# Pooled attention of a fused attention and MoE kernel: 112 + 32 keys per head on array tiles in place of block-diagonal weights

## The chip, the cores and the metric

One NeuronCore of a Trainium2 chip. The time of a kernel is the device time of one execution in microseconds (us), as the median of the runs of one session. The engines are named as in the profile: PE (TensorE matmul), PEld (its weight load), DVE (VectorE), ACT (ScalarE), POOL (GpSimd), SP (SyncE, which here only issues DMAs).

## The reference

The kernel computes an attention layer for 8 batches of 8 heads (576 positions, 64 per head) and, on its output, a gated feed-forward layer of 4608 tokens, 512 wide inside and out, 1536 in the middle. Attention is the sum of two: a pooled one over groups of four positions, and a local one within a distance of 3.

```python
def _attn_ref(q, k, v):
    B, H, S, D = q.shape                       # 8, 8, 576, 64
    factor, scale = 4, 1.0 / np.sqrt(D)
    Sd = S // factor                           # 144 pooled positions
    ...                                        # sm_attn: softmax(scale * q k^T) v
    q_d = q.reshape(B, H, Sd, factor, D).mean(axis=3)   # k_d, v_d alike
    out_up = np.repeat(sm_attn(q_d, k_d, v_d), factor, axis=2)
    mask = np.abs(pos[:, None] - pos[None, :]) < factor
    ...                                        # masked softmax of q k^T, times v
    return out_up + out_local

def _moe_ref(x, w_gate, w_val, w_out):
    gate = np.maximum(x @ w_gate, 0.0)
    return gate * (x @ w_val) @ w_out
```

## The kernel before

**Order.** Nothing is scheduled by the compiler: every engine runs its instructions in the order in which they are emitted, and that order is one long list of tokens, `SEQ` (2338 of them). A token such as `scores/a/0@2` names a step, a pair of heads and a chunk of tokens, and calls one function. The 64 heads are worked on as 32 pairs (two heads side by side: head 0 on partitions 0 to 63, head 1 on 64 to 127); the feed-forward layer works on nine chunks of 512 tokens, and its matmuls (L951, L1295, L1199, L1036) are interleaved token by token with the attention of pairs further on. Four pairs are worked on for each chunk.

**Pairs before the twelfth** use an older form. Their local scores and pooled scores are matmuls over 64 rows, one per head (L621 for the pooled ones with 72 keys, L632 for the local ones, each head in a PSUM bank of its own). Pairs 0 to 3 form their output on other lines (L669, L681); pairs 4 to 7 have denominators and numerators for two heads on 64 columns each (L722, L731, L743, L752). Q and K of the first pairs are turned by matmuls with 64 output columns (L549).

**Pairs from the twelfth on** (`NEW = 12`, twenty pairs) treat both heads in one matmul over all 128 rows, with block-diagonal weights: a weight tile that holds head 0 in its upper left and head 1 in its lower right quarter, zeros elsewhere.

- Loads: Q and K by GpSimd's DMA queue, turned by a DMA transpose on SP's queue (`emit_qkT`, L529). V comes twice: for the local part in fp16 (`emit_load_vb`), and for the pooled part in fp32 (`emit_load_v4`, L520), on SP's queue. Rows 0 to 47 of that tile hold head 0, rows 64 to 111 head 1, each row 12 consecutive positions, so three pooled keys (w = 0, 1, 2).
- Pooling: Q and K by a reduction on VectorE (`emit_pool`, L536) into `qkd`, [128, 2, 144]; V by two additions on GpSimd (`emit_v2`, L573, then `emit_v1`, L581, two instructions of 48 partitions) into `vp`, three block-diagonal weight tiles. K is copied by ScalarE (`emit_kd`, L806, one copy per head) into `kd`, again three block-diagonal tiles of 2 x 48 keys.
- Scores (`emit_scores`): four matmuls for the pooled part (L836: 144 columns for w = 0 and w = 1, 72 for each half of w = 2), then ten for the local part (L840). `flat` is all of PSUM as one row of 8 banks of 512; the pooled results lie at 0 to 215 and 798 to 1013 from the start of bank 4, the local ones between.
- Exponentials on ScalarE (`emit_exp_st`, `emit_exp_pool`), a mask on VectorE (`emit_mask_st`).
- Output (`emit_out_st`): step 0 is `emit_pooled` twice, first for the denominator (weights `four_st`, a block of fours that is loaded from a constant), then for the numerator (weights `vp`), three matmuls of 144 columns each (L867). Step 1 is the local denominator (L882), steps 2 and 3 the local numerator (L887). Then logarithm, inverse and product (`emit_ln_st`, L899; `emit_inv`, L920; `emit_xn_st`, L902) and the sum of the two attentions (`emit_xsum_st`).

Zeros that the block-diagonal tiles need are written once by `emit_zero` (kinds `d` and `v` on VectorE, L813), and tokens `const/2`, `zero/d/*`, `zero/v/*` and `kd/*` in `SEQ` place these steps.

```python
        for w, o, a, n in ((0, 0, 0, SD), (2, SD, 0, 72), (1, 798, 0, SD), (2, 798 + SD, 72, 72)):
            nc.tensor.matmul(
                out=flat[:, lo + o : lo + o + n], lhsT=kd[r2][:, w, :], rhs=qd[:, a : a + n], start=True, stop=True
            )
```

Of the kernel before, what the change touches and what calls it, by code (L numbers as in the profile page):

```python
# [43 lines left out]
next/0/1@0 vd/7/4 qk/b0/1@0 qk/a1/1@0 hg/11/*/7 relu/11/7 next/1/1@0 flip/9 hv/11/*/0 p/1/0@1 gate/11/0 sumhi/0/0@1
v/a/1@0 vc/7/4 num/7/1/7 tr/8/0/1 keep/1/0@1 zero/b/6 ev/8/01A/1 wt/1 v/b/0@0 num/7/0/6 tr/8/1/0 wt/2 den/7/0/4
den/7/1/5 ln/4 sumhi/1/0@1 p/2/0@1 c11//0@1 zs/1.1/0@1 qk/b2/0@1 qk/b2/1@0 p/6/0@1 vd/8/5 ev/8/00A/1 inv xn/6
p/5/0@1 next/0/0@1 keep/2/0@1 vc/8/5 ev/8/10A/0 p/7/0@1 ev/8/11A/0 scores/a/0@1 exp/a1/0@1 xsum/7 keep/3/0@1
hg/0/0@1 qk/b3/1@0 hv/0/0@1 wt/3 relu/0/0@1 qk/a0/0@1 flip/10 qk/a2/0@1 mask/a1/0@1 hg/2/0@1 next/2/0@1 sum/3/0@1
ed/a/0@1 o/a11/0@1 c22//0@1 exp/a0/0@1 mask/a0/0@1 next/1/0@1 p/4/0@1 o/a01/0@1 qk/a3/0@1 zs/1.0/0@1 tn/1/0@1
gate/0/0@1 c21//0@1 o/a10/0@1 ln/a1/0@1 p/3/0@1 flip/11 next/3/0@1 qk/b3/0@1 c12//0@1 relu/2/0@1 qk/b1/0@1 o/a00/0@1  # L50
ln/a0/0@1 inv/a/0@1 pool/b/0@1 xn/a1/0@1 hg/1/0@1 relu/1/0@1 zero/b/1 v2/a/1@1 hg/4/0@1 zero/b/5 hv/1/0@1 gate/1/0@1
hv/2/0@1 xn/a0/0@1 qk/b0/0@1 vd/9/7 vc/9/7 hg/3/0@1 relu/3/0@1 flip/12 gate/2/0@1 xsum/a/0@1 zs/2.0/0@1 scores/b/0@1
exp/b0/0@1 mask/b0/0@1 exp/b1/0@1 mask/b1/0@1 qk/a3/1@1 hv/3/0@1 gate/3/0@1 vd/10/2 ed/b/0@1 zs/3.0/0@1 vc/10/2
# [10 lines left out]
qk/b2/1@1 hg/4/1@1 hg/5/1@1 qk/b1/0@2 xsum/a/1@1 inv/b/1@1 xn/b1/1@1 v/b/0@1 xn/b0/1@1 kd/a1/1@1 v2/b/1@1 v4/b/1@1
qk/b0/0@2 hv/4/1@1 kd/a0/1@1 relu/5/1@1 relu/4/1@1 gate/4/1@1 hv/5/1@1 gate/5/1@1 zero/b/4 v/b/1@1 zero/k/1
qk/b3/0@2 qk/b2/0@2 xsum/b/1@1 up/2.1/0@2 xq/0/0@2 xq/1/0@2 kk/b0/0@2 sq/4.0.0.1/0@2 xq/2/0@2 scores/a/0@2
vh/10.6/0@2 uk/2.1/0@2 sk/4.0.0.1/0@2 sq/4.0.0.2/0@2 sq/4.0.0.5/0@2 sq/4.0.0.6/0@2 sumhi/0/0@2 kk/b1/0@2 vh/4.7/0@2
sf/4.0.0.11/0@2 xq/3/0@2 sk/4.0.0.2/0@2 v2/a/0@2 sq/4.0.0.3/0@2 next/0/1@1 sk/4.0.0.5/0@2 sq/4.0.0.7/0@2 up/2.5/0@2
sumhi/1/0@2 exp/a0/0@2 ed/a/0@2 next/1/1@1 kk/a1/0@2 sf/4.0.0.22/0@2 sq/4.0.0.4/0@2 sf/4.0.0.21/0@2 mask/a0/0@2
sf/4.0.0.12/0@2 gt/4.7.0/0@2 up/2.6/0@2 uk/2.2/0@2 uk/2.5/0@2 sq/0.0.2.1/0@2 sq/0.0.2.5/0@2 sk/0.0.2.5/0@2 sum/2/0@2  # L70
sum/3/0@2 gt/10.6.1/0@2 o/a00/0@2 o/a01/0@2 up/2.7/0@2 sk/0.0.2.1/0@2 uf/2.22/0@2 sq/0.0.2.6/0@2 sk/0.0.2.2/0@2
ln/a0/0@2 inv/a/0@2 pool/b/0@2 next/0/0@2 up/2.2/0@2 o/a10/0@2 sq/0.0.2.3/0@2 sq/0.0.2.2/0@2 sf/0.0.2.11/0@2
sq/0.0.2.7/0@2 v1/a/0@2 after/3/0@2 sf/0.0.2.22/0@2 sf/0.0.2.12/0@2 kd/b0/0@2 o/a11/0@2 xn/a0/0@2 up/2.4/0@2
# [1550 lines left out]
```

## Time and profile before

| | |
|---|---|
| median of 3 runs | 343.01 us (342.77 to 344.65) |
| span of the profiled execution, first to last instruction | 341.8 us |
| the profiled execution's own time | not listed apart from its span; the median of the runs is 1.2 us above it |
| busy in the span | PE 331.0 (97%), DVE 292.9 (86%), ACT 272.1 (80%), POOL 188.6 (55%) |
| instructions | 9062, of them 3410 matmuls |
| granted TensorE clock | 1.00 |
| DMA | 43.91 MB in 162176 packets; HBM read 46.59 MB, written 9.44 MB |

A row of a group reads: line, engine, operation, output and inputs by name, rows*columns of the weight tile, shape, type, count, then busy time of the group, mean ns of one, and idle time of the engine before them with what ended it. A row of the timeline reads: start, length, engine, line, operation, names, shape, count; neighbours of one form are merged. The duration of a matmul goes from its start to the modelled end of its results, and the next one may start well before that. The rows themselves stand in the prediction.

### The profile page before, as it was taken

The page shows a single profiled execution, that of the slowest core. Times are in us where ns is not written, and L with a number is a line of the kernel's source. Part 1 is how long each engine was busy: PE and PEld are TensorE (multiplying, and loading weights), DVE is VectorE, ACT ScalarE, POOL GpSimd, SP SyncE. Part 2 cuts the span into 40 slices and gives each one's busy share as a digit, 9 for nine tenths or more (in the row PEclk, how much of TensorE's full clock was granted, in tenths as well). Part 3 has the DMA queues.
Part 4 walks back from the last instruction along what each step waited for, and adds up shares of the span by engine and source line. Part 5 has one row for each costly group of instructions (what it writes and reads, how often), then busy time and mean ns, then how long its engine had stood idle before and what let it go on. Part 6 is the DMA issues. An engine that isn't in the chain of part 4 may idle for free.

```text
span 341.8 us, 9062 instructions
## 1 busy us (share of the span) xinstructions
PE 331.0 (97%) x3410; PEld 243.5 (71%) x3410; DVE 292.9 (86%) x578; ACT 272.1 (80%) x653; POOL 188.6 (55%) x268
## 2 busy tenths in 40 slices
PE   7899999999999999999999999999999999999995
PEld 3765556657457786878677868787778768888874
DVE  6694689999999898989899989998998898897692
ACT  3878787799997998889889888988898647896842
POOL 8993655929998669849985698675510000000000
PEclk9999999999999999999999999999999999999999
DMA  9999999999999999999999999999300102003013
GB/s 135 165 170 208 185 194 167 150 186 148 168 187 133 192 88 218 128 185 105 220 118 194 92 191 151 189 122 190 51 33 1 63 2 93 3 15 109 3 56 130
DMA packets 162176, 43.91 MB, mean 128 GB/s; under 512 B 147500, under 2 KB 156820, under 8 KB 162132
## 3 DMA queue, kind: packets, MB, share of 16 engines
q0 software_dynamic: 123136, 19.51, 79.5%
q1 hardware_dynamic: 38884, 23.80, 32.3%
q8 instruction: 26, 0.43, 0.5%
q14 instruction: 18, 0.15, 0.1%
q10 hardware_dynamic: 112, 0.02, 0.0%
HBM read 46.59 MB, written 9.44 MB: 164 GB/s over the span
## 4 chain that ended last, share of the span: by engine, by line
PE 79%; DMA 6%; DVE 5%; POOL 4%; ACT 3%; issue 2%; DVEq 0%; ACTq 0%; POOLq 0%
PE ps L1295 24%; PE ps L951 24%; PE ps L1199 17%; DMA qk<-in_k_dram 3%; PE ps L1036 3%; DMA wv_sb<-in_moe_w_val_dram 3%; PE ps L867 2%; POOL qk L463 2%; PE ps L840 2%; PE ps L887 1%; PE ps L882 1%; POOL vw L513 1%; PE ps L836 1%; DVE xo L1030 1%; DVE xT L1175 1%
## 5 line engine op out<-in xcount | busy, mean ns | idle before, releaser
L951 PE MATMUL ps<-xT,wv_sb 128*128 128x512 f16 x352 | 89.4, 379 | 0.0
L951 PEld LDWEIGHTS <-wv_sb 128*128 128x128 f16 x352 | 32.5, 97 | 27.5
L468 POOL DMA_DIRECT2D qk<-in_k_dram x46 | 33.6, 732 | 19.3 <-DMA qkT<-qk 16.3
L1390 DVE SCALAR_TENSOR_TENSOR gT<-r,ps 128x512 f16<-128x512 f16 x55 | 37.5, 682 | 6.1 <-PE ps L951 5.1
L1295 PE MATMUL ps<-xT,qk 128*128 128x256 f16 x240 | 40.9, 272 | 0.0
L468 POOL DMA_DIRECT2D qk<-in_q_dram x46 | 34.0, 740 | 12.1 <-DMA qkT<-qk 7.1
L1306 ACT COPY ps<-ps 128x256 f32<-128x256 f32 x80 | 29.0, 366 | 8.1 <-PE ps L1295 7.4
L1295 PE MATMUL ps<-xT,wg_sb 128*128 128x256 f16 x180 | 33.9, 272 | 1.1 <-DVE xT L1313 0.6
L536 DVE TENSOR_REDUCE qkd<-qkT 128x288 f16<-128x1152 f16 x23 | 30.8, 1338 | 0.0
L486 POOL DMA_DIRECT2D vw<-in_v_dram x40 | 28.9, 732 | 2.3 <-DMA qk<-in_q_dram 1.7
L1311 ACT CAST r<-ps 128x256 f16<-128x256 f32 x55 | 20.2, 367 | 11.0 <-DVE r L1313 6.3
L581 POOL TENSOR_TENSOR vd<-v 48x192 f16<-48x192 f32 x40 | 26.0, 650 | 1.7
L1210 ACT COPY ps<-ps 128x256 f32<-128x256 f32 x54 | 19.4, 366 | 9.1 <-PE ps L1199 7.3
L951 PE MATMUL ps<-xT,wg_sb 128*128 128x512 f16 x104 | 26.1, 380 | 0.5 <-ACT r L960 0.5
L1295 PEld LDWEIGHTS <-qk 128*128 128x128 f16 x240 | 22.2, 97 | 4.8
L573 POOL TENSOR_TENSOR v<-v 112x384 f32<-112x384 f32 (+1 forms) x21 | 22.6, 1074 | 4.0 <-DMA v<-in_v_dram 3.6
L1295 PEld LDWEIGHTS <-xo 128*128 128x128 f16 x240 | 22.5, 97 | 2.9 <-DVE xo L1030 0.2
L1295 PEld LDWEIGHTS <-wg_sb 128*128 128x128 f16 x180 | 17.0, 97 | 10.7 <-issue 3.1
L1295 PE MATMUL ps<-wt,xo 128*128 128x256 f16 x180 | 24.5, 272 | 0.0
L920 ACT ACTIVATE rden<-rden 128x720 f32<-128x720 f32 x28 | 22.5, 803 | 0.8
L1313 DVE TENSOR_TENSOR r<-ps,xT 128x256 f16<-128x256 f32 x44 | 18.1, 418 | 4.4 <-PE ps L1295 3.1
L963 DVE TENSOR_TENSOR gT<-r,ps 128x512 f16<-128x512 f16 x24 | 16.1, 679 | 6.0 <-PE ps L951 3.2
(181 smaller groups left out, 883.8 us busy)
## 6 DMA issues: line engine op xcount, KB each, us to landing
out_dram<-y_sb SPq DMA_DIRECT2D x24, 256.0 KB, 3.8
v<-in_v_dram SPq DMA_DIRECT2D x20, 192.0 KB, 5.1
qk<-in_k_dram POOLq DMA_DIRECT2D x46, 72.0 KB, 5.6
qk<-in_q_dram POOLq DMA_DIRECT2D x46, 72.0 KB, 5.2
vw<-in_v_dram POOLq DMA_DIRECT2D x38, 80.0 KB, 4.5
v<-in_v_dram SPq DMA_DIRECT2D x20, 144.0 KB, 5.2
out_dram<-y_sb SPq DMA_DIRECT2D x22, 128.0 KB, 1.8
vw<-in_v_dram POOLq DMA_DIRECT2D x12, 168.0 KB, 6.2
```

Of the source, the lines that this page charges most:

```text
L468: nc.gpsimd.dma_start(dst.rearrange("p (j h d) -> p j h d", h=2, d=64)[:, :, hh, :], _dap(src, off + hh * S * D, [[D, 96], [NQ * D, NB], [ ...
L486: nc.gpsimd.dma_start(t[lo : lo + 64, j0:j1, lo : lo + 64], _dap(v, base + j0 * QB * D, [[D, 64], [QB * D, j1 - j0], [1, D]]),)
L536: nc.vector.tensor_reduce(out=qkd[hp % 2].rearrange("p i t -> p (i t)"), in_=qkT[hp % 4][:, 0 : 2 * S].rearrange("p (t f) -> p t f", f=4), ...
L573: nc.gpsimd.tensor_tensor(out=m, in0=t[:, :, 0:128], in1=t[:, :, 128:256], op=ALU.add)
L581: nc.gpsimd.tensor_tensor(out=vp[hp % 3][lo : lo + 48, :, lo : lo + 64], in0=m[:, :, 0:64], in1=m[:, :, 64:128], op=ALU.add)
L920: nc.scalar.activation(out=rden, in_=rden, func=AF.Exp, scale=-1.0)
L951: nc.tensor.matmul(out=out, lhsT=w[:, kk, bass.ts(jj, 128)], rhs=xT[:, kk, c * TCH : (c + 1) * TCH], start=(kk == 0), stop=(kk == 3),)
L1199: nc.tensor.matmul(out=out, lhsT=self.left[i][t], rhs=self.right[i][t], start=(i == 1 and t == 0), stop=(t == n - 1), skip_group_check=True,)
L1295: nc.tensor.matmul(out=out, lhsT=self.left[i - 1][k], rhs=self.right[i - 1][k], start=(i == 1 and k == 0), stop=(k == n - 1), skip_group_c ...
L1306: nc.scalar.copy(out=o, in_=x)
L1311: nc.scalar.copy(out=o, in_=self.d if i == 11 else self.a)
L1390: lambda c, jj, b, t: nc.vector.scalar_tensor_tensor(out=gT[c % 2][:, jj, :], in0=tg[t], scalar=0.0, in1=ps[:, b, :], op0=ALU.max, op1=ALU ...
```

## The change

For the twenty pairs from the twelfth on, the pooled part no longer uses block-diagonal tiles. Each head's 144 pooled keys are split into 112 and 32.

- Scores: one matmul per head over its own 64 rows for 112 keys (144 columns), and for the last 32 keys two per head (72 columns, one for each half of the queries), head 0 to partitions 0 to 31, head 1 to 32 to 63. Six matmuls in place of four, with weights straight from `qkd`; `emit_kd`, `kd` and its zeros go.
- Output: denominator and numerator have one matmul per head over 112 keys, to 64 columns each, and one per head over 32 keys on 32 rows. Eight matmuls in place of six. Weights of the denominator are a part of `ones_sb` that is there already (`four_st` and its load go).
- V for the pooled part: 112 partitions with both heads side by side, and 32 partitions per head for the rest: three loads in place of two, rows of 1 KB in place of 3 KB. `emit_v1` is one instruction of 112 partitions in place of two of 48.
- The exponential of the pooled scores covers 112 partitions, and two memsets at the start clear what no load fills. Of the 14 first warming matmuls, one each goes to banks 4 and 5. 48 tokens leave `SEQ`; the order of the others is unchanged.

```diff
+    MK = 112
+    RK = SD - MK
...
-    vp = [t.rearrange("p (w k) -> p w k", k=128) for t in vdfull]
+    vp = [t[:, 0:192].rearrange("p (w d) -> p w d", d=64) for t in vdfull]
...
+        for t in v4n:
+            nc.vector.memset(t[64:MK, 512:768], 0.0)
...
         if hp >= NEW:
+            t = v4n[hp % 2]
+            nc.sync.dma_start(
+                t[0:MK, 0:512].rearrange("p (h x) -> p h x", h=2),
+                _dap(v, off, [[4 * D, MK], [S * D, 2], [1, 4 * D]]),
+            )
             for hh in range(2):
-                lo, n = 64 * hh, 64 - 16 * hh
                 nc.sync.dma_start(
-                    v4n[hp % 2][lo : lo + n], _dap(v, off + hh * S * D, [[12 * D, n], [1, 12 * D]])
+                    t[RK * hh : RK * hh + RK, 512:768],
+                    _dap(v, off + hh * S * D + 4 * MK * D, [[4 * D, RK], [1, 4 * D]]),
                 )
...
         if hp >= NEW:
-            for lo in (0, 64):
-                m = v2full[hp % 2][lo : lo + 48, 0:3]
-                nc.gpsimd.tensor_tensor(
-                    out=vp[hp % 3][lo : lo + 48, :, lo : lo + 64], in0=m[:, :, 0:64], in1=m[:, :, 64:128], op=ALU.add
-                )
+            m = v2full[hp % 2][0:MK, 0:3]
+            nc.gpsimd.tensor_tensor(out=vp[hp % 3][0:MK], in0=m[:, :, 0:64], in1=m[:, :, 64:128], op=ALU.add)
...
-    def emit_kd(hp, hh):
-        lo = 64 * hh
-        nc.scalar.copy(
-            out=kd[hp % 2][lo : lo + 64, :, lo : lo + 48],
-            in_=qkd[hp % 2][lo : lo + 64, 1, :].rearrange("p (k w) -> p w k", w=3),
-        )
...
-        qd = qkd[r2][:, 0, :]
-        for w, o, a, n in ((0, 0, 0, SD), (2, SD, 0, 72), (1, 798, 0, SD), (2, 798 + SD, 72, 72)):
+        heads = [qkd[r2][64 * hh : 64 * hh + 64] for hh in range(2)]
+        for hh, d in enumerate(heads):
             nc.tensor.matmul(
-                out=flat[:, lo + o : lo + o + n], lhsT=kd[r2][:, w, :], rhs=qd[:, a : a + n], start=True, stop=True
-            )
+                out=flat[0:MK, lo + 798 * hh : lo + 798 * hh + SD], lhsT=d[:, 1, 0:MK], rhs=d[:, 0, :], start=True, stop=True
+            )
+        for i in range(2):
+            o = lo + 798 * i + SD
+            for hh, d in enumerate(heads):
+                nc.tensor.matmul(
+                    out=flat[RK * hh : RK * hh + RK, o : o + 72],
+                    lhsT=d[:, 1, MK:SD],
+                    rhs=d[:, 0, 72 * i : 72 * i + 72],
+                    start=True,
+                    stop=True,
+                )
...
     def emit_pooled(hp, lo, weights):
-        for w in range(3):
-            e = ep[hp % 2].rearrange("p (c t) -> p c t", c=2)
-            nc.tensor.matmul(
-                out=flat[:, lo + 798 : lo + 942],
-                lhsT=weights(w),
-                rhs=e[:, :, SD:] if w == 2 else e[:, w, 0:SD],
-                start=(w == 0),
-                stop=(w == 2),
-            )
+        e = ep[hp % 2].rearrange("p (c t) -> p c t", c=2)
+        for rest in range(2):
+            for hh in range(2):
+                a, n = (RK * hh, RK) if rest else (0, MK)
+                nc.tensor.matmul(
+                    out=flat[64 * hh : 64 * hh + 64, lo + 798 : lo + 942],
+                    lhsT=weights(2 if rest else hh)[a : a + n],
+                    rhs=e[a : a + n, :, SD:] if rest else e[0:n, hh, 0:SD],
+                    start=not rest,
+                    stop=bool(rest),
+                )
...
         if i == 0:
-            emit_pooled(hp, den, lambda w: four_st)
+            emit_pooled(hp, den, lambda w: ones_sb[:, 64:128])
             emit_pooled(hp, num, lambda w: vp[hp % 3][:, w, :])
...
-        emit_warm(14, wide=True)
+        for n, bank in ((12, 7), (1, 4), (1, 5)):
+            emit_warm(n, bank, True)
```

More of the change, by code (lines that the diff above doesn't have):

```diff
@@ L44 @@
[L44 to L53, printed above, removed]
@@ L64 @@
[L64 to L73, printed above, removed]
@@ new lines @@
+next/1/1@0 flip/9 hv/11/*/0 p/1/0@1 gate/11/0 sumhi/0/0@1 v/a/1@0 vc/7/4 num/7/1/7 tr/8/0/1 keep/1/0@1 zero/b/6
+ev/8/01A/1 wt/1 v/b/0@0 num/7/0/6 tr/8/1/0 wt/2 den/7/0/4 den/7/1/5 ln/4 sumhi/1/0@1 p/2/0@1 c11//0@1 zs/1.1/0@1
+qk/b2/0@1 qk/b2/1@0 p/6/0@1 vd/8/5 ev/8/00A/1 inv xn/6 p/5/0@1 next/0/0@1 keep/2/0@1 vc/8/5 ev/8/10A/0 p/7/0@1
+ev/8/11A/0 scores/a/0@1 exp/a1/0@1 xsum/7 keep/3/0@1 hg/0/0@1 qk/b3/1@0 hv/0/0@1 wt/3 relu/0/0@1 qk/a0/0@1 flip/10
+qk/a2/0@1 mask/a1/0@1 hg/2/0@1 next/2/0@1 sum/3/0@1 ed/a/0@1 o/a11/0@1 c22//0@1 exp/a0/0@1 mask/a0/0@1 next/1/0@1
@@ new lines @@
+gate/4/1@1 hv/5/1@1 gate/5/1@1 zero/b/4 v/b/1@1 zero/k/1 qk/b3/0@2 qk/b2/0@2 xsum/b/1@1 up/2.1/0@2 xq/0/0@2 xq/1/0@2
+kk/b0/0@2 sq/4.0.0.1/0@2 xq/2/0@2 scores/a/0@2 vh/10.6/0@2 uk/2.1/0@2 sk/4.0.0.1/0@2 sq/4.0.0.2/0@2 sq/4.0.0.5/0@2
+sq/4.0.0.6/0@2 sumhi/0/0@2 kk/b1/0@2 vh/4.7/0@2 sf/4.0.0.11/0@2 xq/3/0@2 sk/4.0.0.2/0@2 v2/a/0@2 sq/4.0.0.3/0@2
+next/0/1@1 sk/4.0.0.5/0@2 sq/4.0.0.7/0@2 up/2.5/0@2 sumhi/1/0@2 exp/a0/0@2 ed/a/0@2 next/1/1@1 kk/a1/0@2
+sf/4.0.0.22/0@2 sq/4.0.0.4/0@2 sf/4.0.0.21/0@2 mask/a0/0@2 sf/4.0.0.12/0@2 gt/4.7.0/0@2 up/2.6/0@2 uk/2.2/0@2
@@ new lines @@
+uk/2.5/0@2 sq/0.0.2.1/0@2 sq/0.0.2.5/0@2 sk/0.0.2.5/0@2 sum/2/0@2 sum/3/0@2 gt/10.6.1/0@2 o/a00/0@2 o/a01/0@2
+up/2.7/0@2 sk/0.0.2.1/0@2 uf/2.22/0@2 sq/0.0.2.6/0@2 sk/0.0.2.2/0@2 ln/a0/0@2 inv/a/0@2 pool/b/0@2 next/0/0@2
+up/2.2/0@2 o/a10/0@2 sq/0.0.2.3/0@2 sq/0.0.2.2/0@2 sf/0.0.2.11/0@2 sq/0.0.2.7/0@2 v1/a/0@2 after/3/0@2 sf/0.0.2.22/0@2
+sf/0.0.2.12/0@2 o/a11/0@2 xn/a0/0@2 up/2.4/0@2 up/2.3/0@2 uf/2.21/0@2 v2/b/0@2 uf/2.11/0@2 uf/2.12/0@2 sq/0.0.2.4/0@2
+sf/0.0.2.21/0@2 pool/a/0@2 sq/1.1.0.1/0@2 sq/1.1.0.5/0@2 sk/1.1.0.5/0@2 scores/b/0@2 v4/b/0@2 vh/0.7/0@2
@@ new lines @@
+sk/1.1.0.1/0@2 sq/1.1.0.6/0@2 v1/b/0@2 exp/b0/0@2 gt/0.7.2/0@2 vh/6.3/0@2 gt/6.3.3/0@2 mask/b0/0@2 sk/1.1.0.2/0@2
+sq/1.1.0.2/0@2 sq/1.1.0.7/0@2 sf/1.1.0.22/0@2 ed/b/0@2 sq/1.1.0.3/0@2 kk/a0/0@2 v4/a/0@2 vh/1.0/0@2 o/b00/0@2
+sf/1.1.0.11/0@2 kk/b1/1@2 sq/1.1.0.4/0@2 sf/1.1.0.21/0@2 o/b01/0@2 sf/1.1.0.12/0@2 ln/b0/0@2 o/b10/0@2 sq/2.2.0.1/1@2
+sq/2.2.0.5/1@2 vh/7.1/0@2 o/b11/0@2 xsum/a/0@2 sk/2.2.0.1/1@2 next/2/0@2 sq/2.2.0.6/1@2 sq/2.2.0.2/1@2 inv/b/0@2
+scores/a/1@2 sk/2.2.0.5/1@2 gt/1.0.0/0@2 qk/a1/1@2 gt/7.1.1/0@2 xn/b0/0@2 sk/2.2.0.2/1@2 v1/a/1@2 up/0.1/1@2 tm/b/0@2
@@ new lines @@
+sf/5.2.0.22/1@2 qk/a2/0@3 vh/5.4/1@2 inv/b/1@2 v4/b/1@2 qk/b0/1@2 qk/b3/0@3 sf/5.2.0.12/1@2 xn/b0/1@2 qk/a3/0@3
+sf/5.2.0.11/1@2 sq/5.2.0.4/1@2 qk/b0/0@3 v4/a/1@2 qk/b2/0@3 v/a/0@3 sf/5.2.0.21/1@2 gt/5.4.0/1@2 xsum/b/1@2
+vh/11.1/1@2 gt/11.1.1/1@2 kk/a1/1@2 qk/b1/0@3 up/2.1/0@3 xq/0/0@3 xq/1/0@3 kk/b0/0@3 sq/4.0.0.1/0@3 xq/2/0@3
+scores/a/0@3 vh/10.6/0@3 uk/2.1/0@3 sk/4.0.0.1/0@3 sq/4.0.0.2/0@3 sq/4.0.0.5/0@3 sq/4.0.0.6/0@3 sumhi/0/0@3 kk/b1/0@3
+vh/4.7/0@3 sf/4.0.0.11/0@3 xq/3/0@3 sk/4.0.0.2/0@3 v2/a/0@3 sq/4.0.0.3/0@3 next/0/1@2 sk/4.0.0.5/0@3 sq/4.0.0.7/0@3
@@ new lines @@
+up/2.5/0@3 sumhi/1/0@3 exp/a0/0@3 ed/a/0@3 next/1/1@2 kk/a1/0@3 sf/4.0.0.22/0@3 sq/4.0.0.4/0@3 sf/4.0.0.21/0@3
+mask/a0/0@3 sf/4.0.0.12/0@3 gt/4.7.0/0@3 up/2.6/0@3 uk/2.2/0@3 uk/2.5/0@3 sq/0.0.2.1/0@3 sq/0.0.2.5/0@3 sk/0.0.2.5/0@3
+sum/2/0@3 sum/3/0@3 gt/10.6.1/0@3 o/a00/0@3 o/a01/0@3 up/2.7/0@3 sk/0.0.2.1/0@3 uf/2.22/0@3 sq/0.0.2.6/0@3
+sk/0.0.2.2/0@3 ln/a0/0@3 inv/a/0@3 pool/b/0@3 next/0/0@3 up/2.2/0@3 o/a10/0@3 sq/0.0.2.3/0@3 sq/0.0.2.2/0@3
+sf/0.0.2.11/0@3 sq/0.0.2.7/0@3 v1/a/0@3 after/3/0@3 sf/0.0.2.22/0@3 sf/0.0.2.12/0@3 o/a11/0@3 xn/a0/0@3 up/2.4/0@3
@@ new lines @@
+exp/a0/1@3 mask/a0/1@3 sq/3.2.1.5/1@3 vh/2.4/1@3 gt/2.4.0/1@3 sk/3.2.1.1/1@3 sq/3.2.1.2/1@3 sk/3.2.1.5/1@3
+sq/3.2.1.6/1@3 uk/0.2/1@3 uk/0.5/1@3 qk/a3/1@3 xsum/b/0@3 o/a00/1@3 o/a11/1@3 sk/3.2.1.2/1@3 next/3/0@3 tm/a/1@3
+up/0.7/1@3 uf/0.22/1@3 sf/3.2.1.11/1@3 o/a01/1@3 v/b/1@3 sq/3.2.1.3/1@3 sq/3.2.1.7/1@3 o/a10/1@3 sf/3.2.1.22/1@3
+kk/b0/1@3 pool/a/1@3 ln/a0/1@3 sf/3.2.1.12/1@3 up/0.2/1@3 inv/a/1@3 xn/a0/1@3 sq/3.2.1.4/1@3 sf/3.2.1.21/1@3
+scores/b/1@3 v/b/0@4 exp/b0/1@3 up/0.3/1@3 sq/5.2.0.1/1@3 ed/b/1@3 sq/5.2.0.5/1@3 sk/5.2.0.5/1@3 up/0.4/1@3
@@ new lines @@
+up/2.1/0@4 xq/0/0@4 xq/1/0@4 kk/b0/0@4 sq/4.0.0.1/0@4 xq/2/0@4 scores/a/0@4 vh/10.6/0@4 uk/2.1/0@4 sk/4.0.0.1/0@4
+sq/4.0.0.2/0@4 sq/4.0.0.5/0@4 sq/4.0.0.6/0@4 sumhi/0/0@4 kk/b1/0@4 vh/4.7/0@4 sf/4.0.0.11/0@4 xq/3/0@4 sk/4.0.0.2/0@4
+v2/a/0@4 sq/4.0.0.3/0@4 next/0/1@3 sk/4.0.0.5/0@4 sq/4.0.0.7/0@4 up/2.5/0@4 sumhi/1/0@4 exp/a0/0@4 ed/a/0@4 next/1/1@3
+kk/a1/0@4 sf/4.0.0.22/0@4 sq/4.0.0.4/0@4 sf/4.0.0.21/0@4 mask/a0/0@4 sf/4.0.0.12/0@4 gt/4.7.0/0@4 up/2.6/0@4
+uk/2.2/0@4 uk/2.5/0@4 sq/0.0.2.1/0@4 sq/0.0.2.5/0@4 sk/0.0.2.5/0@4 sum/2/0@4 sum/3/0@4 gt/10.6.1/0@4 o/a00/0@4
@@ new lines @@
+o/a01/0@4 up/2.7/0@4 sk/0.0.2.1/0@4 uf/2.22/0@4 sq/0.0.2.6/0@4 sk/0.0.2.2/0@4 ln/a0/0@4 inv/a/0@4 pool/b/0@4
+next/0/0@4 up/2.2/0@4 o/a10/0@4 sq/0.0.2.3/0@4 sq/0.0.2.2/0@4 sf/0.0.2.11/0@4 sq/0.0.2.7/0@4 v1/a/0@4 after/3/0@4
+sf/0.0.2.22/0@4 sf/0.0.2.12/0@4 o/a11/0@4 xn/a0/0@4 up/2.4/0@4 up/2.3/0@4 uf/2.21/0@4 v2/b/0@4 uf/2.11/0@4 uf/2.12/0@4
+sq/0.0.2.4/0@4 sf/0.0.2.21/0@4 pool/a/0@4 sq/1.1.0.1/0@4 sq/1.1.0.5/0@4 sk/1.1.0.5/0@4 scores/b/0@4 v4/b/0@4
+vh/0.7/0@4 sk/1.1.0.1/0@4 sq/1.1.0.6/0@4 v1/b/0@4 exp/b0/0@4 gt/0.7.2/0@4 vh/6.3/0@4 gt/6.3.3/0@4 mask/b0/0@4
@@ new lines @@
+sf/5.2.0.11/1@4 sq/5.2.0.4/1@4 qk/b0/0@5 v4/a/1@4 qk/b2/0@5 v/a/0@5 sf/5.2.0.21/1@4 gt/5.4.0/1@4 xsum/b/1@4
+vh/11.1/1@4 gt/11.1.1/1@4 kk/a1/1@4 qk/b1/0@5 up/2.1/0@5 xq/0/0@5 xq/1/0@5 kk/b0/0@5 sq/4.0.0.1/0@5 xq/2/0@5
+scores/a/0@5 vh/10.6/0@5 uk/2.1/0@5 sk/4.0.0.1/0@5 sq/4.0.0.2/0@5 sq/4.0.0.5/0@5 sq/4.0.0.6/0@5 sumhi/0/0@5 kk/b1/0@5
+vh/4.7/0@5 sf/4.0.0.11/0@5 xq/3/0@5 sk/4.0.0.2/0@5 v2/a/0@5 sq/4.0.0.3/0@5 next/0/1@4 sk/4.0.0.5/0@5 sq/4.0.0.7/0@5
+up/2.5/0@5 sumhi/1/0@5 exp/a0/0@5 ed/a/0@5 next/1/1@4 kk/a1/0@5 sf/4.0.0.22/0@5 sq/4.0.0.4/0@5 sf/4.0.0.21/0@5
@@ new lines @@
+mask/a0/0@5 sf/4.0.0.12/0@5 gt/4.7.0/0@5 up/2.6/0@5 uk/2.2/0@5 uk/2.5/0@5 sq/0.0.2.1/0@5 sq/0.0.2.5/0@5 sk/0.0.2.5/0@5
+sum/2/0@5 sum/3/0@5 gt/10.6.1/0@5 o/a00/0@5 o/a01/0@5 up/2.7/0@5 sk/0.0.2.1/0@5 uf/2.22/0@5 sq/0.0.2.6/0@5
+sk/0.0.2.2/0@5 ln/a0/0@5 inv/a/0@5 pool/b/0@5 next/0/0@5 up/2.2/0@5 o/a10/0@5 sq/0.0.2.3/0@5 sq/0.0.2.2/0@5
+sf/0.0.2.11/0@5 sq/0.0.2.7/0@5 v1/a/0@5 after/3/0@5 sf/0.0.2.22/0@5 sf/0.0.2.12/0@5 o/a11/0@5 xn/a0/0@5 up/2.4/0@5
+up/2.3/0@5 uf/2.21/0@5 v2/b/0@5 uf/2.11/0@5 uf/2.12/0@5 sq/0.0.2.4/0@5 sf/0.0.2.21/0@5 pool/a/0@5 sq/1.1.0.1/0@5
@@ new lines @@
+uk/2.2/0@6 uk/2.5/0@6 sq/0.0.2.1/0@6 sq/0.0.2.5/0@6 sk/0.0.2.5/0@6 sum/2/0@6 sum/3/0@6 gt/10.6.1/0@6 o/a00/0@6
+o/a01/0@6 up/2.7/0@6 sk/0.0.2.1/0@6 uf/2.22/0@6 sq/0.0.2.6/0@6 sk/0.0.2.2/0@6 ln/a0/0@6 inv/a/0@6 pool/b/0@6
+next/0/0@6 up/2.2/0@6 o/a10/0@6 sq/0.0.2.3/0@6 sq/0.0.2.2/0@6 sf/0.0.2.11/0@6 sq/0.0.2.7/0@6 v1/a/0@6 after/3/0@6
+sf/0.0.2.22/0@6 sf/0.0.2.12/0@6 o/a11/0@6 xn/a0/0@6 up/2.4/0@6 up/2.3/0@6 uf/2.21/0@6 v2/b/0@6 uf/2.11/0@6 uf/2.12/0@6
+sq/0.0.2.4/0@6 sf/0.0.2.21/0@6 pool/a/0@6 sq/1.1.0.1/0@6 sq/1.1.0.5/0@6 sk/1.1.0.5/0@6 scores/b/0@6 v4/b/0@6
@@ L290, in _np_stacked @@
     out[:, 576:704] = same
-    out[:, 704:832] = 4.0 * (same & (i[:, None] < 48))
     return out
@@ L1121, in emit_warm @@
             nc.tensor.matmul(
-                out=ps[:, 7, :] if wide else ps[:, bank, 264:512],
+                out=ps[:, bank, :] if wide else ps[:, bank, 264:512],
                 lhsT=zero_sb[:, 0:128],
```

377 lines of the change are left out of this document (161 added, 216 removed).

## The prediction

> **What bounds the kernel now.** I read the page's busy time, slices and chain first, then busy time by stretch, then what the matmul engine waited for.
>
> ```profile
> PE 331.0 (97%) x3410; PEld 243.5 (71%) x3410; DVE 292.9 (86%) x578; ACT 272.1 (80%) x653; POOL 188.6 (55%) x268
> PEclk9999999999999999999999999999999999999999
> PE 79%; DMA 6%; DVE 5%; POOL 4%; ACT 3%; issue 2%; DVEq 0%; ACTq 0%; POOLq 0%
> ```
>
> TensorE is busy 97% of the span, at the full granted clock in every slice, and carries 79% of the chain that ended last. An average can hide a stage with another limit, so the stretches of the twenty changed pairs come next. Their score matmuls are those of L836; columns after the stretch are its length, then busy us (instructions) of PE, PEld, DVE, ACT, POOL, then clock, DMA share and GB/s.
>
> ```profile
> L836 PE MATMUL ps<-qkd,cst_sb x80: 196/212/228, 97.3 to 264.7; 128*128 128x144 f16 x40, 128*128 128x72 f16 x40
> 131.00:166.00 35.00, 34.78 (x345) 26.36 (x344) 32.05 (x59) 30.41 (x72) 27.54 (x40) 1.00 1.45 159
> 201.00:236.00 35.00, 35.00 (x350) 26.55 (x347) 32.45 (x60) 30.15 (x72) 26.41 (x40) 1.00 1.34 171
> ```
>
> The scores of the changed pairs run from 97.3 to 264.7 us. In the middle of that, TensorE is busy 34.78 and 35.00 of 35 us. VectorE has 2.6 to 3 us free in each 35, ScalarE 4.6 to 4.9, GpSimd over 7. So within these pairs, what is put on TensorE's queue is paid nearly in full, and what is taken from the others is paid nothing. What TensorE waited for there (us, times, longest) is small:
>
> ```profile
> PE ps L1295 <- DVE xT L1313: 0.6, 2, 0.4
> PE ps L1295 <- ACT ps L1306: 0.4, 1, 0.4
> PE ps L1295 <- ACT r L960: 0.4, 1, 0.4
> PE ps L887 <- DVE gT L1390: 0.3, 1, 0.3
> ```
>
> **TensorE: columns saved.** Starts in the timeline are the clock to use, because a matmul's duration contains its tail and several tails overlap. The first column is the start, the second the length of the merged row; the last row gives the beat of a 512-column matmul, (1.90 - 0.38)/7 = 0.217 us, with 0.38 the row L951 of the page (379 ns).
>
> ```profile
> L951 PE MATMUL ps<-xT,wv_sb 128*128 128x512 f16 x352 | 89.4, 379 | 0.0
> 203.72 0.35 PE L836 MATMUL ps<-qkd,cst_sb 128*128 128x144 f16 x4
> 203.91 0.45 PE L840 MATMUL ps<-qkT,kk 128*128 128x58 f16 x10
> 209.22 0.35 PE L867 MATMUL ps<-att 128*128 128x144 f16 x3
> 209.41 0.35 PE L867 MATMUL ps<-att,vd 128*128 128x144 f16 x3
> 209.60 0.41 PE L882 MATMUL ps<-att,one_st 128*128 128x290 f16 x2
> ...
> 38.84 1.04 PE L951 MATMUL ps<-xT,wg_sb 128*128 128x512 f16 x4
> 39.80 0.31 PE L722 MATMUL ps<-att,ones_sb 112*64 112x288 f16 x2
> 39.95 0.23 PE L731 MATMUL ps<-att,ones_sb 72*64 72x72 f16 x4
> 40.02 0.29 PE L722 MATMUL ps<-att,ones_sb 112*64 112x288 f16 x2
> 40.15 0.23 PE L731 MATMUL ps<-att,ones_sb 72*64 72x72 f16 x4
> 40.21 0.29 PE L743 MATMUL ps<-att,vw 112*64 112x96 f16 x6
> 40.34 0.23 PE L752 MATMUL ps<-att,vd 72*64 72x72 f16 x4
> 40.51 1.90 PE L951 MATMUL ps<-xT,wv_sb 128*128 128x512 f16 x8
> ...
> 42.89 0.38 PE L549 MATMUL ps<-cst_sb,qk 96*64 96x120 f16 x8
> 43.20 0.25 PE L621 MATMUL ps<-qkd 64*72 64x144 f16 x2
> 43.29 0.29 PE L632 MATMUL ps<-qkT 64*128 64x96 f16 x6
> 43.42 0.23 PE L621 MATMUL ps<-qkd 64*72 64x144 f16 x2
> 43.48 0.29 PE L632 MATMUL ps<-qkT 64*128 64x96 f16 x6
> 43.70 0.61 PE L951 MATMUL ps<-xT,wg_sb 128*128 128x512 f16 x2
> ```
>
> Per pair today, four pooled score matmuls take 203.91 - 203.72 = 0.19 us, and six pooled output matmuls 209.60 - 209.22 = 0.38, so 0.062 for 144 columns and about 0.031 for 72. The later rows are of earlier pairs, which already use part of the array. Two 288-column matmuls on 64 columns each (one per head) take 40.15 - 40.02 = 0.13 us, the time of one (288/512 of 0.217 is 0.12): tiles of the two heads run side by side. Those on 64 rows do so too: six of 96 columns start 43.29 to 43.42, 0.13 us, three beats of 0.04. The new scores are one such pair of 144 columns and two of 72: 0.062 + 2 x 0.031 = 0.125, a saving of 0.065. The new outputs are eight of 144 in four pairs, 0.25 for 0.38: a saving of 0.125. Together 0.19 us per pair, if all of them pair up.
>
> **TensorE: switches added.** The same rows show the price of changing the tile shape. Four 512-column matmuls from 38.84 end their beats at 38.84 + 4 x 0.217 = 39.71; the first tiled one starts at 39.80, so 0.09 us is lost on entry. From there to the next full matmul at 40.51 is 0.71 us, for work of 0.13 (each L722 pair, by the second) + 0.07 + 0.13 + 0.06 + 0.13 + 0.06 = 0.58: 0.13 lost, on a first pair that is slower (0.15 for 0.13) and on the exit. That is 0.22 for two switches. The other excursion: four pairs of 120 columns (0.05 each) from 42.89 end at 43.09, the 64-row tiles start at 43.20, 0.11 lost although both sides are tiles; 43.20 to 43.70 is 0.50 for 2 x 0.06 + 6 x 0.04 = 0.36 to 0.37 of work, 0.13 lost. So a switch costs 0.09 to 0.13; I take 0.11, the mean of the two on the first excursion.
>
> Now count them. Scores go from the full array to 64 rows (112 columns), to 64 rows by 32 columns, and back to the full array for the local scores: three. Outputs go to 64-column tiles for the denominator over 112 keys, to 32-row tiles for its rest, back to 64 columns for the numerator, again to 32 rows, then to the full array: five. Eight per pair, 8 x 0.11 = 0.88, where there were none. Net 0.88 - 0.19 = 0.69 us per pair, 13.8 us over twenty pairs. Of the eight, the rows show entries, exits and one change between tile shapes; none from 64 to 32 rows or columns. The Trainium skill, TensorEngine Tiling (Array Packing), Tiling Modes under Key Properties, says that changing the tiling mode drains TensorE, whereas changing only the tile does not. By that rule all eight are paid, as in my sum; were only entries and exits paid, the net would be 4 x 0.11 - 0.19 = 0.25 per pair.
>
> **The rest of the change, and what covers it.** None of these is on TensorE.
>
> ```profile
> L806 ACT COPY cst_sb<-qkd 64x144 f16<-64x144 f16 x40 | 12.3, 308 | 2.6 <-DVE qkd L536 2.2
> L581 POOL TENSOR_TENSOR vd<-v 48x192 f16<-48x192 f32 x40 | 26.0, 650 | 1.7
> L520 SPq DMA_DIRECT2D v<-in_v_dram x40: 471/574/1359, 23.3 to 235.5; - x40
> SPq L529 <- DMA qk<-in_q_dram: 62.6, 9, 34.9
> 5.39 0.45 DVE L443 MEMSET xo<- 32x128 uint32 x3
> 6.82 0.56 DVE L563 CAST qkT<-ps 128x384 f16<-128x384 f32 x1 [0.99 <-PE ps L549]
> 94.73 0.63 ACT L806 COPY cst_sb<-qkd 64x144 f16<-64x144 f16 x2
> ```
>
> ScalarE loses 40 copies, 12.3 us; GpSimd's pooling add becomes one instruction instead of two, 20 x 0.65 = 13 us less if a 112-partition one takes as long as a 48-partition one. Both engines have room, so I take no gain from them directly. SyncE issues three loads of V per pair instead of two, 20 x 0.57 = 11.5 us more. Behind them on its queue stand the transposes of Q and K (L529) and the stores, and that queue itself sat 62.6 us waiting for Q loads; TensorE waited for none of its transposes in these pairs. I take nothing; if that cover went, 0.57 per pair would be the upper end. Two more memsets at the start (48 partitions by 256 floats, under 0.3 us each from 0.15 for 128) fit in VectorE's 0.99 us of idle time before 6.82. Three loads' bytes are the two loads' bytes.
>
> Indirectly there is a gain: the four waits above add up to 1.7 us in five events, and each hides up to a tail more (0.379 - 0.217 = 0.16 us), so at most 2.5 us. The two ScalarE waits lie close behind the copies at 94.73, which go; the VectorE waits shrink when TensorE comes later. I take 1.5, bounds 0 and 2.5.
>
> **Sum.** 13.8 - 1.5 = 12.3 us. The profiled span of 341.8 us becomes 354.1; the median of the runs, 343.01, is 1.2 us above that span, and I carry this over: 355.3 us. With a switch at 0.09 and 2.5 recovered, 10.6 - 2.5 = 8.1 gives 351.1; at 0.13 and nothing recovered, 17.0 gives 360.0.
>
> **Rivals.** *Tiles of one bank take turns* (0.20). All the 72-column scores of a half go to one PSUM bank from two row tiles, and so do the two 32-row outputs; in the rows above, row tiles write to different banks (the code of L621 and L632 gives each head its own), so nothing shows the case. If they wait for each other, 2 x 0.031 + 2 x 0.062 = 0.19 per pair comes back and no columns are saved: 0.88 x 20 - 1.5 = 16.1, 359.1 us. The Trainium skill, TensorEngine Tiling (Array Packing), Restrictions and Gotchas, says that different row tiles cannot use the same PSUM bank at once; here their column ranges differ too, which the page does not treat, so the rule may not bite.
>
> *Only entries and exits are paid* (0.06): 5.0 - 1.5 = 3.5, 346.5 us. Against it stands the 0.11 at 43.09, a change from one tile shape to another.
>
> *No tiles at all* (0.04): the change does not do what it says, the small matmuls run one after another on the full array, and no switch is paid. Scores take 2 x 0.062 + 4 x 0.031 = 0.25 for 0.19, outputs 8 x 0.062 = 0.50 for 0.38, so 0.18 x 20 - 1.5 = 2.1, 345.1 us. The rows with 64 rows or 64 columns speak against it.
>
> *Faster* (0.05): the switch is hidden. If weights for the next shape load while the last matmuls stream, a switch costs nothing, the 0.19 remains: -3.8 - 1.5 = -5.3, 337.7 us. The point that decides is 0.19/8 = 0.024 us per switch, a quarter of the lowest one read above; and both excursions lie on a full queue, where hiding would have shown.
>
> **How the numbers follow.** The forecast has 0.65. The range runs from 349 to 362: the whole 351.1 to 360.0 of the forecast and most of the turn-taking case (359.1, and 0.13 x 8 x 20 = 20.8, 363.8, at its dearest); left out are the two small cases near 346, the fast one and part of the tails, some 0.18. About half a per cent (1.7 us) is what a measurement of this kernel can tell from no change, so under 341.3 is faster and over 344.7 slower. Faster: 0.05. Same: 0.02, the cheap ends of the two cases near 346. Slower: 0.93.
>
> **What would show it.** In the changed profile, from the first pooled score matmul to the first local one should be 0.125 + 2 x 0.11 = 0.35 us instead of 0.19, with another 0.1 of standstill ahead of it; from the first pooled output to the next full matmul 0.25 + 4 x 0.11 = 0.69 instead of 0.38. A stretch of four pairs, now about 35 us, should take about 38. Starts of two heads' matmuls a few ns apart in the 72-column scores and the 32-row outputs refute the turn-taking case. The forecast is wrong if the starts across a switch are no further apart than the columns, or if the excess appears but the stretch does not lengthen, which would mean that TensorE had slack I did not see.

## The result and the profile after

The changed kernel takes 356.66 us (355.80 to 357.12), the kernel before 343.56 us in the same session. The ratio is 1.0361, 95% interval 1.0326 to 1.0395: slower by 3.6%, 11.2 to 13.6 us. The prediction was 355.3 us, range 349 to 362.

The profile page of the changed kernel: busy time by engine, and the chain that ended last by engine.

```profile
span 354.5 us, 9194 instructions
PE 344.7 (97%) x3490; PEld 242.7 (68%) x3490; DVE 294.0 (83%) x575; ACT 263.5 (74%) x613; POOL 174.3 (49%) x248
PE 77%; DVE 7%; DMA 5%; POOL 4%; issue 3%; ACT 2%; SPq 0%; DVEq 0%; POOLq 0%; ACTq 0%
```

The span grew by 12.7 us (341.8 to 354.5) and TensorE's busy time by 13.7, while ScalarE lost 8.6 and GpSimd 14.3 us of work. By stretches of the same middle part (columns as before), TensorE stays full and the others have more room.

```profile
131.00:166.00 35.00, 34.72 (x341) 24.56 (x339) 30.77 (x56) 26.39 (x59) 22.70 (x34) 1.00 1.26 142
201.00:236.00 35.00, 35.00 (x333) 24.14 (x331) 29.90 (x55) 26.80 (x62) 23.41 (x35) 1.00 1.35 148
```

The timeline of TensorE around one pair's pooled scores (L820, L826), then around another's pooled outputs (L863; the merged rows hold the two matmuls over 112 keys and the two over 32):

```profile
210.65 0.38 PE L1291 MATMUL ps<-xT,wg_sb 128*128 128x256 f16 x2
210.96 0.27 PE L820 MATMUL ps<-qkd 64*112 64x144 f16 x2
211.16 0.24 PE L826 MATMUL ps<-qkd 64*32 64x72 f16 x4
211.34 0.43 PE L834 MATMUL ps<-qkT,kk 128*128 128x58 f16 x9
...
216.43 0.38 PE L1291 MATMUL ps<-xT,qk 128*128 128x256 f16 x2
216.74 0.43 PE L863 MATMUL ps<-att,ones_sb 112*64 112x144 f16 x4
217.10 0.43 PE L863 MATMUL ps<-att,vd 112*64 112x144 f16 x4
217.47 0.42 PE L878 MATMUL ps<-att,one_st 128*128 128x290 f16 x2
```

From the first pooled score to the first local one it is 211.34 - 210.96 = 0.38 us, where it was 0.19, and the two 256-column matmuls ahead (0.217 of beats from 210.65, so to 210.87) are followed by 0.09 of standstill. From the first pooled output to the next full matmul it is 217.47 - 216.74 = 0.73, where it was 0.38, again with 0.09 ahead of it. By the starts in nanoseconds over all twenty pairs, medians: scores 93 ahead + 371 + 12 on the first full matmul behind = 476, against 191 before; outputs 93 + 726 + 11 = 830, against 375. That is 0.285 and 0.455 us per pair, 0.74 together, 14.8 us over twenty pairs. The span grew by 12.7, which is 2.1 less.

### The profile page after: what moved, and what is told of

Read it like the earlier page. It is cut to its first block, busy times and chain, and to the rows that moved or that the text cites. A ratio compares the mean times of both kernels' runs of the same rounds, so it can differ in the third digit from the quotient of the medians.

```text
span 354.5 us, 9194 instructions
## 1 busy us (share of the span) xinstructions
PE 344.7 (97%) x3490; PEld 242.7 (68%) x3490; DVE 294.0 (83%) x575; ACT 263.5 (74%) x613; POOL 174.3 (49%) x248
## 4 chain that ended last, share of the span: by engine, by line
PE 77%; DVE 7%; DMA 5%; POOL 4%; issue 3%; ACT 2%; SPq 0%; DVEq 0%; POOLq 0%; ACTq 0%
PE ps L1291 22%; PE ps L947 20%; PE ps L1195 16%; PE ps L863 4%; DMA qk<-in_q_dram 3%; PE ps L834 2%; PE ps L546 2%; DMA qkT<-qk 2%; PE ps L883 1%; PE ps L878 1%; DVE gT L1386 1%; POOL vw L478 1%; PE ps L1032 1%; POOL qk L460 1%; PE ps L820 1%
## 5 line engine op out<-in xcount | busy, mean ns | idle before, releaser
L1386 DVE SCALAR_TENSOR_TENSOR gT<-r,ps 128x512 f16<-128x512 f16 x55 | 37.5, 682 | 12.8 <-PE ps L947 12.2
L1520 POOL COPY seen<-att 112x1 f16<-112x1 f16 x16 | 5.0, 314 | 47.4 <-DVE att L856 47.4
L570 POOL TENSOR_TENSOR v<-v 112x384 f32<-112x384 f32 (+1 forms) x21 | 21.6, 1027 | 4.8 <-DMA v<-in_v_dram 4.7
```

The source lines that it names most:

```text
L570: nc.gpsimd.tensor_tensor(out=m, in0=t[:, :, 0:128], in1=t[:, :, 128:256], op=ALU.add)
L1386: lambda c, jj, b, t: nc.vector.scalar_tensor_tensor(out=gT[c % 2][:, jj, :], in0=tg[t], scalar=0.0, in1=ps[:, b, :], op0=ALU.max, op1=ALU ...
```

## Experiments

Theory: each change of tile shape is paid on TensorE's queue. Its main rival: the loss lies in the rest of the change (third V load, wider addition, shifted order). All ratios are to the kernel before, run on the same chip at the same time.

**Scores back on the full array.**

```diff
-        heads = [qkd[r2][64 * hh : 64 * hh + 64] for hh in range(2)]
...
+        qd = qkd[r2][:, 0, :]
+        for w, o, a, n in ((0, 0, 0, SD), (2, SD, 0, 72), (1, 798, 0, SD), (2, 798 + SD, 72, 72)):
+            nc.tensor.matmul(
+                out=flat[:, lo + o : lo + o + n], lhsT=kk[r2][:, w, :], rhs=qd[:, a : a + n], start=True, stop=True
+            )
```

> The changed kernel, with its pooled scores again as four matmuls on the full array (144, 72, 144, 72 columns), their weights taken from the local block-diagonal tile that lies there anyway: pooled scores are not the reference's, nothing else is left out. Theory (every change of tile shape is paid on TensorE's queue): three switches go, and 0.19 us of columns come back for the tiled form's 0.37 from first score to first local one plus 0.09 ahead of it; 0.28 us per pair, 5.7 us over twenty pairs, so about 351 us. Rival (the loss lies in the other parts: the third V load, the wider addition, the order of waits): the time stays within 2 us of the changed kernel's 356.7.

Measured: 352.45 us, ratio 1.0225 (1.0189 to 1.0260), which is 1.36% or 4.7 us under the changed kernel's 1.0361, where theory had 5.7. The rival's two microseconds are exceeded.

**Outputs back on the full array.**

```diff
+        e = ep[hp % 2][0:MK].rearrange("p (c t) -> p c t", c=2)
+        for w in range(3):
+            nc.tensor.matmul(
+                out=flat[:, lo + 798 : lo + 942],
+                lhsT=weights(w),
+                rhs=e[:, :, 0:72] if w == 2 else e[:, w, 0:SD],
+                start=(w == 0),
+                stop=(w == 2),
+            )
...
+            emit_pooled(hp, den, lambda w: one_st[0:MK])
+            emit_pooled(hp, num, lambda w: vdfull[hp % 3][0:MK, 64 * (w % 2) : 64 * (w % 2) + 128])
```

> The changed kernel, with its pooled outputs as three matmuls of 144 columns on the full array for the denominator and three for the numerator (112 rows, 128 columns of weights that lie there anyway): pooled outputs are not the reference's. Theory: five switches go; 0.73 us from first pooled output to the next full matmul plus 0.09 ahead of it become 0.375; 0.45 us per pair, 9.1 us, so about 347.5 us. Rival (loss in the other parts): within 2 us of 356.7.

Measured: 349.2 us, ratio 1.0139 (1.0111 to 1.0167): 2.2% or 7.6 us under the changed kernel, where theory had 9.1. In both runs a part of what the queue gained went into waits. Starts between the first and the last changed pair that come over 40 ns later than the columns ahead allow, the usual loss at a change of shape set aside, add up to 4.1 us in the changed kernel's trace, and to 5.8 and 6.0 in the traces of these two.

**Both.**

> Both edits together: all that the change does but the tiles (three V loads, one wider addition, no K copies, no zeros), with as many columns on TensorE as before; pooled scores and outputs are not the reference's. Theory: what is left against the kernel before is the relief of ScalarE and GpSimd alone, 0 to 2.5 us, so 341 to 343.5 us. Rival (loss in the other parts): stays above 346.

Measured: 343.72 us, ratio 0.9987 (0.9952 to 1.0022). Without the tiles the rest of the change makes no difference that shows, -1.6 to +0.8 us. The two savings (4.7 and 7.6) add up to nearly the whole of 12.9 us. The rival falls: the loss is the tiles. The run gives the sum of the relief and of what the rest costs; a gain at the top of what I allowed (2.5 us) is excluded for that sum, not for the relief by itself.

**Fewer switches, same matmuls.** Per pair, the four outputs over 112 keys first, then the four over 32.

```diff
+            for rest in range(2):
+                emit_pooled(hp, den, lambda w: ones_sb[:, 64:128], rest)
+                emit_pooled(hp, num, lambda w: vp[hp % 3][:, w, :], rest)
```

> The changed kernel with the eight pooled outputs in another order: the four over 112 keys (denominator, then numerator), then the four over 32 keys. Two of the five switches go, the columns are the same. Theory: a switch between tile shapes with one pair of matmuls in each costs 0.115 us, so two save 0.23 us per pair, 4.6 us, about 352 us. Rival 1 (only entries and exits are paid, the inner ones come from the narrow matmuls themselves): no change, 356.7. Rival 2 (the numerator's wait for its bank, which now holds up the denominator's rest too, eats the gain): 355 or more.

Measured: 354.86 us, ratio 1.0294 (1.0235 to 1.0354), about 2.3 us under the changed kernel, with intervals that overlap. The timeline says more than the total. One pair's outputs, then another's where a wait falls in, then what ended the waits:

```profile
189.19 0.25 PE L862 MATMUL ps<-att,ones_sb 112*64 112x144 f16 x2
189.27 0.23 PE L862 MATMUL ps<-att,vd 112*64 112x144 f16 x2
189.43 0.25 PE L862 MATMUL ps<-att,ones_sb 32*64 32x144 f16 x2
189.52 0.22 PE L862 MATMUL ps<-att,vd 32*64 32x144 f16 x2
189.68 0.39 PE L1291 MATMUL ps<-xT,wg_sb 128*128 128x256 f16 x2
...
178.84 0.25 PE L862 MATMUL ps<-att,ones_sb 112*64 112x144 f16 x2
179.73 0.25 PE L862 MATMUL ps<-att,vd 112*64 112x144 f16 x2 [0.65 <-DVE gT L1386]
...
PE ps L862 <- DVE gT L1386: 1.7, 4, 0.6
```

Undisturbed, the outputs take 189.68 - 189.19 = 0.49 us in place of 0.73: the two removed switches are worth 0.24 us per pair, as the theory has it. But in four of the twenty pairs, each the first of a chunk, the numerator has to wait until VectorE has read its bank (L1386), and TensorE, less held up than in the changed kernel, waits longer there. By starts, those four hold-ups come to 2.5 us, where the changed kernel has 0.9 in three. So rival 2 took part of the gain, and rival 1 falls. That it explains all of the missing gain is not shown: the interval of the total is wider than what is missing.

Where VectorE lost the time in the pair shown is visible just before: the mask (L856) took 1.48 us, where the median of that row is 0.45, while GpSimd added V (L570, then L577).

```profile
177.15 1.48 DVE L856 TENSOR_TENSOR att<-att,zero_sb 128x576 f16<-128x576 f16 x1
178.55 0.41 DVE L1309 TENSOR_TENSOR r<-ps,xT 128x256 f16<-128x256 f32 x1
178.99 0.69 DVE L1386 SCALAR_TENSOR_TENSOR gT<-r,ps 128x512 f16<-128x512 f16 x1
...
177.29 1.01 POOL L570 TENSOR_TENSOR v<-v 112x384 f32<-112x384 f32 x1
178.25 0.82 POOL L577 TENSOR_TENSOR vd<-v 112x192 f16<-112x192 f32 x1
```

The Trainium skill, SBUF — State Buffer, under SBUF: two separate sides, says that a VectorE operation with two SBUF inputs and a GpSimd operation that reads SBUF exclude each other for a whole instruction. The mask has two SBUF inputs, and its excess of 1.0 us matches the 1.01 us of the addition beside it. Of the other masks of this trace, sixteen ran with no addition beside them and took 0.44 to 0.46 us, and one that ran beside the whole of another such addition took 1.36. Two more, of 0.92 and 1.15 us, ran mostly while GpSimd issued DMAs, beside which other masks took 0.45: for these two no cause is shown. Why the mask is the one held up, though its record starts 0.14 us before the addition's, stays open, and no run here took the addition away.

**Switches alone, in the kernel before.** One, then both of its 72-column score matmuls are split into two halves of 64 columns: nothing else of the change is in it.

```diff
-            nc.tensor.matmul(
-                out=flat[:, lo + o : lo + o + n], lhsT=kd[r2][:, w, :], rhs=qd[:, a : a + n], start=True, stop=True
-            )
+            for c0, c1 in ((0, 64), (64, 128)) if w == 2 and a == 0 else ((0, 128),):   # both: if w == 2
+                nc.tensor.matmul(
+                    out=flat[c0:c1, lo + o : lo + o + n],
+                    lhsT=kd[r2][:, w, c0:c1],
...
```

> The kernel before, with one of its two 72-column pooled score matmuls split into two halves of 64 columns of the array, side by side: the same results and the same columns per unit of time, plus one round trip from the full array to 64-column tiles and back per pair. Theory (a drain at each change, and a slower first pair): 0.21 to 0.22 us per round trip, 4.3 us over twenty pairs, about 347.8 against 343.5. Rival (a switch is hidden when only one pair of matmuls is in the tile shape, and what the changed kernel loses comes from its 32-row shapes): under 1 us.

> The same with both 72-column matmuls split: two round trips per pair. Theory: twice the loss of one round trip, 8.6 us, about 352 us. Rival: TensorE has slack that takes up part of a small loss, so that the first round trip costs less than the second; then the first gives under 3 us and the second over 4 more.

Measured: one round trip 349.45 us, ratio 1.0153 (1.0100 to 1.0207), +5.3 us (3.4 to 7.1); two 351.82 us, ratio 1.0221 (1.0183 to 1.0260), +7.6 us (6.3 to 8.9). The scores of the kernel with two trips:

```profile
207.83 0.38 PE L1300 MATMUL ps<-xT,wg_sb 128*128 128x256 f16 x2
208.05 0.70 PE L837 MATMUL ps<-qkd,cst_sb 128*128 128x144 f16 x6
208.68 0.29 PE L845 MATMUL ps<-qkT,kk 128*128 128x58 f16 x4
```

208.68 - 208.05 = 0.63 us for the columns that took 0.19: 0.22 per round trip, as expected, 9 us for forty. Some 84% of that reached the time with two trips; with one the interval holds anything from 75% up, and its middle, 5.3 us, is over the 4.4 that the switches cost. At least the profiled execution of that run was late for another reason: its first changed scores start at 99.33 us, 2.1 us later than in the kernel before, ahead of every added switch. The rival that a lone pair of matmuls hides its switch falls, and so does the other rival, in which the first trip should cost under 3 us.

**The relief alone.** The kernel before without its copies of K.

```diff
-    PAIR_STEPS["kd"] = diag(emit_kd)
+    PAIR_STEPS["kd"] = lambda hp, a: None
```

> The kernel before without the 40 copies of pooled K on ScalarE (the block-diagonal tiles stay zero, so all pooled scores are 0 and the pooled softmax is uniform). It prices the relief alone. Theory: the TensorE waits behind ScalarE close to 95 to 99 us go, 0.5 to 1.5 us faster than before, 342 to 343. Rival (ScalarE sets the pace somewhere that the waits do not show): over 3 us faster. Rival (nothing waits for these copies): within 0.3 us.

Measured: 342.77 us, ratio 0.9954 (0.9927 to 0.9982), 0.6 to 2.5 us faster. It bounds what the copies cost: little. No TensorE wait named them, but one stood right behind them. In the kernel before, ScalarE comes to its L960 only after two copies (0.63 us from 94.73), and TensorE waits for that; without the copies the same matmuls follow with no wait (last two rows, of the run without copies):

```profile
95.27 1.06 ACT L960 ACTIVATE r<-ps 128x512 f16<-128x512 f32 x2
96.39 0.81 PE L1295 MATMUL ps<-wo_sb,gT 128*128 128x256 f16 x6 [0.36 <-ACT r L960]
...
94.24 1.07 ACT L960 ACTIVATE r<-ps 128x512 f16<-128x512 f32 x2
95.49 0.71 PE L1295 MATMUL ps<-wo_sb,gT 128*128 128x256 f16 x5
```

By the starts this one wait costs 0.52 us. It is there in the three traces with the copies on ScalarE (the kernel before and the two with round trips) and in none of the other seven.

**A version that this points to: the copies on GpSimd.**

```diff
-        nc.scalar.copy(
+        nc.gpsimd.tensor_copy(
             out=kd[hp % 2][lo : lo + 64, :, lo : lo + 48],
```

> The kernel before with the 40 copies of pooled K on GpSimd instead of ScalarE, at the same places of the order: the same results. It is the version that the run without these copies points to (0.5% under before). Theory (TensorE's queue sets the time, and ScalarE's relief is worth what that run gave): 0 to 1.6 us faster than before if GpSimd's queue carries 40 more instructions of about 0.4 us (16 us more on 188.6 of 341.8). Rival (GpSimd's queue holds up the scores of the same pair, or its work slows VectorE's): 2 us or more slower.

Measured: 374.6 us, ratio 1.0870 (1.0830 to 1.0910). The expectation missed by 30 us, on the rival's side. TensorE's largest wait of the kernel, and the queue of GpSimd ahead of one copy:

```profile
PE ps L836 <- POOL cst_sb L806: 23.5, 6, 6.0
196.51 0.19 POOL L1465 COPY seen<-xo 128x1 f16<-128x1 f16 x1 [6.42 <-DVE xo L1030]
198.72 0.87 POOL L806 COPY cst_sb<-qkd 64x144 f16<-64x144 f16 x2 [2.03 <-PE ps L887]
```

The copy itself costs 0.31 us; it stands behind a step that makes GpSimd wait on purpose for VectorE (6.4 us here), waits 2.0 us more itself, which the profile puts down to TensorE, and the scores stand behind it. Counting GpSimd's busy time, as I did, misses that. The waits are not the whole loss: the granted clock fell as well. Around one of the long waits (5.3 us, to 142.77), with the columns stretch, length, busy us and instructions of PE, clock, DMA share and GB/s:

```profile
136.00:142.00 6.00, 1.49 (x11) 0.99 1.78 189
142.00:148.00 6.00, 5.23 (x28) 0.50 1.58 108
148.00:150.00 2.00, 2.00 (x16) 0.83 0.17 10
150.00:152.00 2.00, 2.00 (x23) 1.00 0.00 0
```

Over the span TensorE is busy 340.4 us for the same 3410 matmuls that took 331.0, so some 9 us more of work stand beside the 23.5 of waits. No version that keeps the results beats the kernel before for certain.

## Why the prediction was right, point by point

- **What bounds the kernel.** Right, and now shown from both sides: work put on TensorE alone (two trips, 9 us) came out at 6.3 to 8.9 us, and work taken from the others alone at 0.6 to 2.5 us for the copies and nothing that shows for all of it together.
- **Columns saved.** Right. In the reordered kernel the eight outputs take 0.49 us: four beats of 0.062 make 0.25, two switches at 0.09 make 0.18, and 0.06 is left for two slower first pairs. A turn of 32-row pairs one after another would add 0.12, for which there is no room.
- **Switches added.** The count of eight was right. The size was a little low: I took 0.11, and 0.74 + 0.19 = 0.93 over eight is 0.116. The parts differ. Entries are about 93 ns (91 to 96 in the twenty pairs), exits from a shape that held two pairs of matmuls 90 to 99, but a change after a single pair costs 112 to 122, and about 135 after the 112-column scores. This is the slower first pair of the prediction: with only one pair per shape it is paid each time. Load times of the weights run alike (L820 122 ns for 112 columns, L863 104 for 64); whether they are the cause was not tried.
- **1.5 us recovered.** The size is near: 14.8 us were added and 12.7 arrived, so 2.1 were recovered. The reason was half right, and part of the size is luck. The waits of TensorE in the changed pairs:

```profile
PE ps L1291 <- DVE xT L1309: 0.7, 1, 0.7
PE ps L863 <- DVE gT L1386: 0.6, 2, 0.3
PE ps L1291 <- DVE r L1309: 0.2, 1, 0.2
PE ps L947 <- DVE xT L759: 0.2, 1, 0.2
```

The ScalarE waits (0.8 us of idle time) are gone, as forecast. Those for VectorE did not shrink but went from 0.9 to 1.7 us, so the recorded idle time is 1.7 us as before.

Where the 2.1 us lie can be read from the starts. The first changed scores start at 97.25 us before and at 96.14 after: 1.1 us are won ahead of every changed matmul. Of these, 0.5 is the wait behind the copies at 96.39, the relief that the prediction named. The rest lies ahead of 44 us, where the kernel before loses up to 0.5 us at a time to loads of K and V. Such waits come and go between versions with the same work there (the reordered kernel has three, the changed one none), so this is not known to come from the change. From the first changed scores to the last, 14.1 us were added over nineteen pairs and 13.1 arrived (167.4 and 180.5 us): 1.0 won. There the late starts, counted as above, add up to 4.9 us before, 4.1 after and 6.4 with the tiles taken out of the changed kernel. The last two differ only in what stands on TensorE's queue, so TensorE coming later hides some 2.3 us; and since 6.4 is more than 4.9, the rest of the change seems to cost waits rather than save them. These are single traces, and even ahead of the first changed pair those of the changed and the reordered kernel, with the same work there, lie 0.8 us apart (96.14 and 96.90).
- **Why the sum came so close.** The switches cost 1.0 us more than forecast (14.8 for 13.8) and 0.6 us more came back (2.1 for 1.5), so the two errors offset each other in part. And 0.7 of the 2.1 lies ahead of 44 us, where nothing shows that the change did it. The mechanism was right; that the sum came within half a microsecond of the span is luck.
- **Turn-taking rival (0.20).** It fell: 0.49 us leaves no room, and in the trace the heads' 72-column scores start 3 to 5 ns apart though they write to one bank. The Trainium skill, TensorEngine Tiling (Array Packing), Restrictions and Gotchas, forbids different row tiles the same bank at once; with different columns as well, these traces show no turn-taking.
- **Entries and exits only (0.06)** fell with the reordered kernel: two inner switches were worth 0.24 us. **No tiles (0.04)** and **hidden switch (0.05)** fell with the timeline.
- **Third V load, wider addition, two memsets at nothing.** Not contradicted. The kernel with both parts back on the full array has them together with the relief, at -1.6 to +0.8 us. The copies alone are worth 0.6 to 2.5 us, so by the middle values (0.9987 against 0.9954) the rest costs 1.1 us, and by the two intervals together anything from about -0.4 to 2.7 us.
- **What would show it.** Forecast 0.35 and 0.69 us, found 0.38 and 0.73; a stretch of four pairs about 38 us for 35: by the starts of the scores 37.6 (173.41 to 210.96) for 35.2 (168.56 to 203.72).
